# Attention with a capped MoE behind it: two units' sums from the exps, the last unit scaled early, products held back, late rows laid at once

## The chip, the cores and the metric

The kernel runs on one core of one Trainium2 chip. Its engines work side by side and wait for each other by semaphores: TensorE (PE in the profile; its weight loads are PEld), VectorE (DVE), ScalarE (ACT), GpSimd (POOL), and SyncE (SP), which issues most DMAs. The metric is the device time of one execution in microseconds, a median over runs.

## The reference

```python
def _attn_ref(q, k, v, cap):                       # 8 x 12 x 448 x 64
    scores = scale * np.matmul(q, k.transpose(0, 1, 3, 2))
    scores = cap * np.tanh(scores / cap)
    scores = scores - np.max(scores, axis=-1, keepdims=True)
    attn = np.exp(scores)
    attn = attn / (np.sum(attn, axis=-1, keepdims=True) + 1e-09)
    return np.matmul(attn, v)

def _moe_ref(x, w_gate, w1, w2, capacity):         # 3584 x 768, 8 experts, F 1024, capacity 80
    logits = x @ w_gate
    expert_idx = np.argmax(logits, axis=1)
    probs = softmax(logits)                        # written out there
    gate_w = probs[np.arange(N), expert_idx]
    out = np.zeros((N, D), dtype=np.float32)
    for e in range(E):
        tok_idx = np.where(expert_idx == e)[0]
        if len(tok_idx) > capacity:
            keep = np.argpartition(-gate_w[tok_idx], capacity)[:capacity]
            tok_idx = tok_idx[keep]
        h = np.maximum(x[tok_idx] @ w1[e], 0.0)
        out[tok_idx] = gate_w[tok_idx, None] * (h @ w2[e])
    return out
```

All 3584 tokens pass through attention and the gate. Of each expert only the tokens with the 80 highest gate weights pass through its two layers; all other rows of the output are zero.

## The kernel before

**Units.** Attention is cut into 24 units: a unit is four heads of one of the eight batches, three units a batch. For a unit TensorE computes the scores (`sc`, lines 1065 and 1073) in seven blocks of keys; ScalarE takes their tanh (line 1074) and exp (line 1078) into the tile `e`. One turn later TensorE multiplies `e` with V (`av`, line 1093, and the rests of the keys, line 1123) and with ones (`sp`, lines 1101 and 1121), which gives the softmax's row sums. To spare TensorE, GpSimd first adds the three full blocks of keys of each head pair (`esum`, tile `t`, lines 1084 and 1086), so that line 1101 multiplies one block instead of three. VectorE turns the sums into reciprocals (`sums`, tiles `st`, `rc`, `r`), scales `av` into `x` (`scaled`, line 1144) and transposes `x` into rows (`turned`, `xb`), which DMAs write to DRAM (`xs`).

**Order by hand.** The order of the work of one unit is the string `STEPS`: q scores, e exp, p GpSimd's sums, a the product with V, t the ones product over the blocks, r the rests, s reciprocals, n scaling, b a slot for the background. Behind the last unit `LAST` does the same, and there q is a step of the first expert's first layer (`begin`) and h makes a second copy of the ones (`again`: a matmul and a copy on ScalarE, `ones2`).

**Background.** After every third unit a gate runs: logits (`lgp`, line 1169), a transposition (`lt`, line 1183), the gate's small arithmetic on VectorE (`gate_math`, with a write of the gate weights `gd` at line 330), and the ranking of the batch's tokens. Ranking compares keys on VectorE (`gb`, line 414) and counts them with products of one column on TensorE (`pd`, line 420), whose result VectorE adds (`dfc`). These are steps in the lists `urgent`, `low` and `bg`, each with a cost in nanoseconds, a mark of what it does to a shared PSUM bank (`use`: 0 and 1 for TensorE's steps, -1 for the VectorE step that frees the bank) and a gap in slots. `background` hands them out in the slots; it keeps a model of TensorE's time (`clock[0]`) and VectorE's (`clock[1]`). In the last units such a step waits in the list while the model says that VectorE isn't there yet.

**Experts.** Six experts' rows are computed in the end. The rows of four are known from the first five batches: GpSimd gathers them by indirect DMAs (`xge`, line 708) and VectorE transposes them (`xt`, line 611). The last two experts wait for the last batch: `slots`, `compact` (`pcp` on TensorE, lines 681 and 684), `indices` (`ga`, `gi`, lines 689 and 692), the gathers `xgv` (three of 32 rows an expert, then the gate weights `gtv`), and `lay`, which transposes (line 1387), rounds on ScalarE (`xh`, line 1388) and subtracts (`xl`, line 1389). TensorE works through a list of 84 chunks (`hp` first layer, `yp` second layer, line 767); VectorE and ScalarE prepare two chunks ahead where weights are split into two parts (`whb` and `wha`, line 755; `wlb` and `wla`, line 757; `tlv`, line 806, is the same for the turned hidden rows). The `hp` tiles behind the first expert lie in the PSUM banks that `av` held.

The lines around the change, cut:

```python
STEPS = ("q0 e3 a00 b q1 q2 r0 b e0 p00 a10 a01 b q3 q4 r2 b e1 p01 t a11 b q5 r1 s q6 e2 p10 p11 a02 n0 a12 n1 b").split()
LAST = ("e3 a00 a10 q a01 a11 b r0 h q t b r2 a02 r1 s a12 q b q b q b q b").split()
```

Of the kernel before, what the change touches and what calls it, by code (L numbers as in the profile page):

```python
# [7 lines left out]
F32 = mybir.dt.float32  # L8
# [4 lines left out]
ALU = mybir.AluOpType  # L13
# [35 lines left out]
WMORE = 6  # L49
AHEAD = 2  # L50
WHOLE = (4, 3)
PLACE = (1900, 2300, 1900, 2400, 2000, 3500)
# [60 lines left out]
def attn_moe(ctx, tc, q2, k, v, cap, wg, w1, w2, capacity, ct, out):  # L113
# [875 lines left out]
    def vector(cost):  # L989

        clock[1] = max(clock) + cost
    st = {"laid": set(), "banks": ["misc"], "held": False}

# [24 lines left out]
    with ExitStack() as a2:  # L1018
# [77 lines left out]
        def total_of(u):  # L1096

            for i in range(2):
                for g in range(4):
                    w = slice(HQ * i, HQ * i + HQ)  # L1100
                    nc.tensor.matmul(st["sp", u][32 * g:32 * g + 32, w], ones[:, 0:32], st["es", u, g // 2][:, g % 2, w], start=False, stop=False)  # L1101

# [68 lines left out]
        def gate(b):  # L1171
# [14 lines left out]
            def math():  # L1186
                cs = slice(b * NC, (b + 1) * NC)
                lt = st["lt", b][:, :, :, 0:E]
                if b < OB:
                    st["math", b] = gate_math(sm, lt, b, kc[:, cs], oh[:, cs], b, us[:, cs], cms[:, cs])  # L1190
                else:
                    ws = slice(b * NC - OCOL, (b + 1) * NC - OCOL)
                    st["math", b] = gate_math(sm, lt, b, kc[:, cs], oh[:, cs], b, None, cmn[:, ws], ohv[:, ws], nc.sync if b < B - 2 else nc.scalar)
            def end(pd):
# [7 lines left out]
            def later():  # L1202
                st["math", b][2]()
                if b < OB:
                    steps = list(ranks(krow, gp, misc, b, acc, dfc, 0, 0, []))
                else:
                    steps = list(ranks(krow, gp, misc, b, acc2, dfc2, CAND, OCOL, [e * SL for e in range(E)]))
                if b == OB - 1:
                    kept = list(prune(krow, gp, misc))
                    n = next(i for i, x in enumerate(kept) if x[0] == 4000)  # L1210
                    steps = [*steps[0:2], kept[0], *steps[2:5], kept[1], *steps[5:8], kept[2], *steps[8:10], *kept[3:n], *steps[10:], *kept[n:]]
                bg.extend(apart(steps))
                now[2] = now[0]
                ready_at[2] = clock[1]
# [22 lines left out]
        def background(quota, took=2330, slack=1e9):  # L1237
# [6 lines left out]
            for q, last in ((urgent, 1), (low, 3), (bg, 2)):  # L1244
                while q and quota > 0:
                    cost, f, gap = q[0]
                    if gap == "ordered":
                        if not st.get("ordered"):
                            break
                        gap = 1  # L1250
                    n = getattr(f, "uses", None)
                    if n in (0, 1) and st["held"]:
                        break
                    if quota < 1e8:
                        if now[0] < now[last] + gap or (gap and n in (0, 1) and slack < 1e8 and clock[0] < ready_at[last]):
                            break
                        if max(clock) + cost > clock[0] + slack:
                            return
                    q.pop(0)
                    quota -= cost  # L1260
                    if n in (1, -1):
                        st["held"] = n == 1
                    vector(cost)
                    now[last] = now[0]
                    ready_at[last] = clock[1]
                    f()

        def laid(v):
# [22 lines left out]
        STEPS = ("q0 e3 a00 b q1 q2 r0 b e0 p00 a10 a01 b q3 q4 r2 b e1 p01 t a11 b q5 r1 s q6 e2 p10 p11 a02 n0 a12 n1 b").split()  # L1291
        LAST = ("e3 a00 a10 q a01 a11 b r0 h q t b r2 a02 r1 s a12 q b q b q b q b").split()
        TURNS = (1, 2, 3, 4, 5, 6, 0)
        RUNS = ((1, 3), (3, 5), (5, 7), (0, 1))
        for w in range(NU + 1):
# [15 lines left out]
            for i, x in enumerate(todo):  # L1311
# [9 lines left out]
                elif k_ == 'p':  # L1321
                    esum(w, *a_)
                elif k_ == 'a' and w:
# [7 lines left out]
                elif k_ == 'h':  # L1331
                    again()
                elif k_ == 'n' and 1 <= w < NU:
                    scaled(w - 1, a_[0])
                    if a_[0] == 1:
                        turned(w - 1, 0)
# [10 lines left out]
    st["banks"].append("sp")  # L1347
    for f in range(2):
        scaled(last_u, f)
    gate(B - 1)  # L1350
# [31 lines left out]
    def lay(v, i):  # L1382
        if i == 0:
            xv[v] = [fp.tile([128, KD, SL], d, name=f"x{k}{v}", tag=f"x{k}", bufs=n) for k, d, n in (("h", F32R, 2), ("l", F32R, 2), ("t", F32, 1))]
        xh, xl, xt = xv[v]
        w = slice(32 * i, 32 * i + 32)
        nc.vector.transpose(xt[:, :, w], fin["xg", v, i].rearrange("p (j c) -> p j c", c=32))
        nc.scalar.copy(xh[:, :, w], xt[:, :, w])
        nc.vector.tensor_tensor(xl[:, :, w], xt[:, :, w], xh[:, :, w].bitcast(F32), op=ALU.subtract)

    def chain():
# [3 lines left out]
        for v in range(NPRE, NV):  # L1395
            for i in range(3):
                bg.append((100, lambda v=v, i=i: fetch(v, i), 0))
            for i in range(3):
                bg.append((700, lambda v=v, i=i: lay(v, i), 3 * int(i == 0)))
        bg.append((800, lambda: fin.update(c=compare(fr, fin["tk"][:, 0:NPRE])), 0))  # L1400
# [101 lines left out]
```

## Time and profile before

| | us |
|---|---|
| median of 3 runs | 511.26 (510.77 to 513.09) |
| the profiled execution | 514.92 |
| its span, first to last instruction | 513.0 |
| TensorE busy | 478.0 (93%) |
| ScalarE busy | 364.2 (71%) |
| VectorE busy | 283.3 (55%) |
| GpSimd busy | 239.2 (47%) |
| mean granted TensorE clock | 0.981 |

The span is 1.9 us shorter than the execution. "Idle before" in brackets tells how long an engine stood before an instruction and what ended the wait; "issue" means that the profile shows nothing that ended it. A granted clock of 1.00 is 2.4 GHz, 0.5 is 1.2 GHz; a stretch that holds some of both shows a mean. Matmuls overlap, so the time that a group takes is the distance from its start to the next group's start. Fp32 matmuls leave two records each.

### The profile page before, as it was taken

To read this page: it belongs to the slowest core of one execution; us is meant where nothing else is said; L and a number is where in the kernel's file an instruction comes from. 1 tells how busy PE (TensorE), PEld (TensorE's weight loads), DVE (VectorE), ACT (ScalarE), POOL (GpSimd) and SP (SyncE) were. 2 spreads that over 40 slices of the span, in tenths; PEclk is the share of its full clock that TensorE was granted. 3 is DMA by queue.
4 is the path that set the end of the run, shared out by engine and by line. 5 is a ranking of instruction groups with operands and counts; after the bars stand their busy time and mean duration, and the time that the engine had idled before them with its cause. 6 is when DMAs were issued, how large, how long until landed. Compare 5 with 4: busy or idle time off the path is not lost.

```text
span 513.0 us, 18283 instructions
## 1 busy us (share of the span) xinstructions
PE 478.0 (93%) x7954; PEld 242.7 (47%) x7954; DVE 283.3 (55%) x753; ACT 364.2 (71%) x359; POOL 239.2 (47%) x164
## 2 busy tenths in 40 slices
PE   5799999999999999989999989999779999988992
PEld 1244444445444544444455435444334545545782
DVE  1033463365256556535878594587642747368881
ACT  4999899899889889968999978885011111256871
POOL 0666655646656656544665663587500014420000
PEclk9999999999999999989999999999989999998997
DMA  6966687685698668518456772945856889799820
GB/s 165 238 157 177 167 218 190 180 249 160 175 226 245 166 175 228 155 54 228 120 121 157 172 204 75 250 158 179 264 177 229 273 255 382 245 377 316 248 88 25
DMA packets 67608, 100.89 MB, mean 197 GB/s; under 512 B 12176, under 2 KB 49968, under 8 KB 67520
## 3 DMA queue, kind: packets, MB, share of 16 engines
q1 hardware_dynamic: 66016, 96.39, 64.8%
q0 software_dynamic: 1440, 3.25, 2.2%
q8 instruction: 64, 1.05, 0.9%
q14 instruction: 24, 0.20, 0.1%
q10 hardware_dynamic: 64, 0.00, 0.0%
HBM read 76.11 MB, written 23.80 MB: 195 GB/s over the span
## 4 chain that ended last, share of the span: by engine, by line
PE 79%; DVE 10%; DMA 4%; ACT 3%; issue 2%; SPq 1%; ACTq 0%; POOL 0%; POOLq 0%; DVEq 0%
PE sc L1073 22%; PE av L1093 19%; PE hp L767 10%; PE yp L767 7%; PE sp L1101 4%; PE av L1123 3%; PE lgp L1169 3%; PE sc L1065 3%; DMA w<-in_w_dram 2%; PE sp L1121 2%; PE pd L420 2%; ACT e L1074 2%; DVE x L1144 1%; DVE xb L1153 1%; DMA xge<-xs,gi 1%
## 5 line engine op out<-in xcount | busy, mean ns | idle before, releaser
L1074 ACT ACTIVATE e<-sc,scl 128x896 f32<-128x896 f32 x168 | 163.9, 1006 | 32.3 <-PE sc L1073 27.0
L1078 ACT ACTIVATE e<-e,capt 128x1792 f32<-128x1792 f32 x96 | 153.3, 1598 | 0.0
L1084 POOL TENSOR_TENSOR t<-e 128x896 f32<-128x896 f32 x48 | 101.1, 2107 | 99.8 <-ACT e L1078 98.7
L1073 PE MATMUL sc<-qt,kt 64*32 64x448 f32 x2304 | 134.7, 554 | 8.8 <-DMA qt<-in_q_dram 4.7
L1093 PE MATMUL av<-e,vr 128*32 128x224 f32 x2304 | 130.1, 359 | 2.4 <-DVE x L1144 2.4
L1086 POOL TENSOR_TENSOR t<-t,e 128x896 f32<-128x896 f32 x48 | 101.2, 2107 | 45.1 <-PE sc L1073 26.2
L1093 PEld LDWEIGHTS av<-e,vr 128*32 128x32 f32 x2304 | 67.8, 110 | 63.4 <-issue 20.1
L1131 DVE STREAM_TRANSPOSE st<-sp 128x448 f32<-128x448 f32 x24 | 15.5, 647 | 121.3 <-PE sp L1121 121.3
L1073 PEld LDWEIGHTS sc<-qt,kt 64*32 64x32 f32 x2304 | 32.8, 106 | 66.2 <-issue 42.4
L414 DVE TENSOR_SCALAR_CACHE_REDUCE gb<-krow,kc 112x896 bf16<-112x896 f32 (+16 forms) x59 | 52.6, 938 | 0.2 <-PE pd L420 0.2
L767 PE MATMUL hp<-w,xt 128*96 128x512 f32 x96 | 45.4, 618 | 2.7 <-issue 2.7
L824 POOL DMA_INDIRECT out_dram<-ysv,si x6 | 5.6, 938 | 83.4 <-ACT ysv L823 75.6
L1123 PE MATMUL av<-e,vr 64*32 64x224 f32 x384 | 41.2, 350 | 0.0
L1123 PE MATMUL av<-e,vx 64*32 64x224 f32 x384 | 40.9, 350 | 0.0
L767 PE MATMUL yp<-w,thv 128*96 128x384 f32 x96 | 32.3, 488 | 0.0
L1121 PE MATMUL sp<-e,ones 64*32 64x224 f32 x384 | 27.8, 350 | 2.8 <-ACT ones L1108 2.8
L1123 PEld LDWEIGHTS av<-e,vr 64*32 64x32 f32 x384 | 19.8, 107 | 21.9 <-issue 15.6
L1144 DVE TENSOR_TENSOR x<-av,r 128x448 f32<-128x448 f32 x48 | 27.7, 618 | 2.4
L1153 DVE STREAM_TRANSPOSE xb<-x 128x448 f32<-128x448 f32 x48 | 28.1, 624 | 0.8
L767 PEld LDWEIGHTS hp<-w,xt 128*96 128x96 f32 x96 | 15.2, 168 | 24.9 <-issue 24.9
L757 DVE TENSOR_TENSOR wlb<-w,whb 128x768 fp32r<-128x768 f32 x24 | 21.8, 952 | 4.8 <-ACT whb L755 4.4
L1101 PE MATMUL sp<-t,ones 128*32 128x224 f32 x384 | 23.5, 359 | 0.0
(263 smaller groups left out, 529.4 us busy)
## 6 DMA issues: line engine op xcount, KB each, us to landing
w<-in_w_dram SPq DMA_DIRECT2D x36, 512.0 KB
w<-in_w_dram SPq DMA_DIRECT2D x48, 384.0 KB
vr<-in_v_dram SPq DMA_DIRECT2D x24, 512.0 KB
out_dram<-zero SPq DMA_DIRECT2D x14, 768.0 KB
xs<-xb SPq DMA_DIRECT2D x32, 336.0 KB
kt<-in_k_dram SPq DMA_DIRECT2D x46, 224.0 KB
qt<-in_q_dram SPq DMA_DIRECT2D x46, 224.0 KB
vx<-in_v_dram SPq DMA_DIRECT2D x48, 32.0 KB
```

What stands on the lines that cost most here:

```text
L414: nc.vector.tensor_scalar(g, krow[:, x:y], kp, 0.0, op0=ALU.is_ge, op1=ALU.add, accum_out=a)
L767: nc.tensor.matmul(ps[nn][:, 0:m] if isinstance(ps, tuple) else ps[:, nn, 0:m], a[:, kk, :], bb[:, nn * m:(nn + 1) * m], start=(kk == 0 an ...
L1073: nc.tensor.matmul(ps[32 * m:32 * m + 32, h, :S], st["k", u][w, pr, y:y + 32], st["q", u][w, pr], start=True, stop=True)
L1074: nc.scalar.activation(st["e", u][:, 2 * x:2 * x + 2], ps[:, :, :S], AF.Tanh, scale=scl)
L1078: nc.scalar.activation(e, e, AF.Exp, scale=capt)
L1084: nc.gpsimd.tensor_tensor(t1, e[:, 0:2], e[:, 2:4], op=ALU.add)
L1086: nc.gpsimd.tensor_tensor(st["es", u, pr], st["es", u, pr], e[:, 4:6], op=ALU.add)
L1093: nc.tensor.matmul(st["av", u, i][32 * g:32 * g + 32, HQ * f:HQ * f + HQ], st["v", u][:, g // 2, g % 2, c, 32 * f:32 * f + 32], chunk_of(u ...
L1101: nc.tensor.matmul(st["sp", u][32 * g:32 * g + 32, w], ones[:, 0:32], st["es", u, g // 2][:, g % 2, w], start=False, stop=False)
L1121: nc.tensor.matmul(st["sp", u][32 * g:32 * g + 32, HQ * i:HQ * i + HQ], st["ones"][w, 0:32], e, start=(part == 0), stop=(part == 1))
L1123: nc.tensor.matmul(st["av", u, i][32 * g:32 * g + 32, HQ * f:HQ * f + HQ], last_of(u, pr, h, i)[w, 32 * f:32 * f + 32], e, start=False, st ...
L1153: nc.vector.transpose(st["xt", b][:, :, j, :], st["x", u][:, f].rearrange("p (a b) -> p a b", b=32))
```

## The change

1. Units 20 and 23 (`DIRECT`) have no sums by GpSimd. TensorE's ones product (`total_of`) takes the three blocks of exps itself, 24 matmuls instead of 8.
2. `LAST` scales the last unit (`n0 n1`) behind its last product with V, in the loop; before, it was done after the loop, behind what the lists had put on VectorE by then. The write of the gate weights of batch 6 goes from ScalarE's queue to SyncE's, and the small VectorE steps ahead of it move from the gate to behind the first count of that batch's ranking.
3. A TensorE step of the background on a shared bank (mark 0 or 1) now waits in its list, in every unit, until the model's TensorE time has reached the modelled end of the last VectorE step marked -1 and, where the step has a gap, the end of the list's last step. Before, this held for steps with a gap in the last units alone.
4. `lay` does an expert's three transposes and three roundings in one step and one subtraction over all 96 rows in a second one.

By 3 the counts' products of two batches stand further back on TensorE: those of the tenth unit's turn (`pd_6`) behind two more score blocks and rests, those of the sixteenth (`pd_14`) behind two products with V, two score blocks and rests. In the last units the logits and one transposition stand one slot later, and behind the last unit most products stand one chunk later, among them `pcp`.

```diff
@@ constants
+DIRECT = (20, 23)
@@ total_of
             for i in range(2):
-                for g in range(4):
-                    w = slice(HQ * i, HQ * i + HQ)
-                    nc.tensor.matmul(st["sp", u][32 * g:32 * g + 32, w], ones[:, 0:32], st["es", u, g // 2][:, g % 2, w], start=False, stop=False)
+                w = slice(HQ * i, HQ * i + HQ)
+                for c in range(NK if u in DIRECT else 1):
+                    for g in range(4):
+                        e = chunk_of(u, g // 2, c, g % 2)[:, w] if u in DIRECT else st["es", u, g // 2][:, g % 2, w]
+                        nc.tensor.matmul(st["sp", u][32 * g:32 * g + 32, w], ones[:, 0:32], e, start=False, stop=False)
@@ gate, math
-                    ... nc.sync if b < B - 2 else nc.scalar)
+                    ... nc.sync if b < B - 1 else nc.scalar)
@@ gate, later
-                st["math", b][2]()
+                if b != B - 2:
+                    st["math", b][2]()
...
-                bg.extend(apart(steps))
+                steps = apart(steps)
+                if b == B - 2:
+                    n = next(i for i, x in enumerate(steps) if i > 1 and getattr(x[1], "uses", None) == -1)
+                    steps.insert(n + 1, (1000, st["math", b][2], 0))
+                bg.extend(steps)
@@ background
-                        if now[0] < now[last] + gap or (gap and n in (0, 1) and slack < 1e8 and clock[0] < ready_at[last]):
+                        if now[0] < now[last] + gap or (n in (0, 1) and clock[0] < max(st["read"], ready_at[last] if gap else 0)):
                             break
...
                     f()
+                    if n == -1:
+                        st["read"] = clock[1]
@@ the loop over units
-        LAST = ("e3 a00 a10 q a01 a11 b r0 h q t b r2 a02 r1 s a12 q b q b q b q b").split()
+        LAST = ("e3 a00 a10 q a01 a11 b r0 h q t b r2 a02 r1 s a12 q n0 n1 b q b q b q b").split()
...
                 elif k_ == 'p':
-                    esum(w, *a_)
+                    if w not in DIRECT:
+                        esum(w, *a_)
...
-                elif k_ == 'n' and 1 <= w < NU:
+                elif k_ == 'n' and w:
                     scaled(w - 1, a_[0])
-                    if a_[0] == 1:
+                    if a_[0] == 1 and w < NU:
@@ after the loop
-    for f in range(2):
-        scaled(last_u, f)
@@ lay
-        w = slice(32 * i, 32 * i + 32)
-        nc.vector.transpose(xt[:, :, w], fin["xg", v, i].rearrange("p (j c) -> p j c", c=32))
-        nc.scalar.copy(xh[:, :, w], xt[:, :, w])
-        nc.vector.tensor_tensor(xl[:, :, w], xt[:, :, w], xh[:, :, w].bitcast(F32), op=ALU.subtract)
+        if i == 1:
+            nc.vector.tensor_tensor(xl, xt, xh.bitcast(F32), op=ALU.subtract)
+            return
+        for k3 in range(3):
+            w = slice(32 * k3, 32 * k3 + 32)
+            nc.vector.transpose(xt[:, :, w], fin["xg", v, k3].rearrange("p (j c) -> p j c", c=32))
+            nc.scalar.copy(xh[:, :, w], xt[:, :, w])
@@ chain
-            for i in range(3):
-                bg.append((700, lambda v=v, i=i: lay(v, i), 3 * int(i == 0)))
+            bg.append((1500, lambda v=v: lay(v, 0), 3))
+            bg.append((700, lambda v=v: lay(v, 1), 1))
```

How the built order of the engines changes is shown at three places; line numbers are those of each kernel, so after the change they are up to 14 higher. First ScalarE behind the last unit's exps, before the change: `tau` belongs to the gate of batch 6, `gd` is the write of its weights, `ones` the second copy of the ones.

```order
L1078 ACTIVATE e_5413<-e_5413,capt 128x1792
L1078 ACTIVATE e_5413<-e_5413,capt 128x896
L304 ACTIVATE tau_5643<-d_5642 112x32
L330 DMA gd<-grow 4x32 x3
L330 DMA gd<-grow 4x16
L1108 COPY ones_5739<-ones_5737 128x32
L396 COPY krow<-psk_5802 112x448
```

And after the change:

```order
L1079 ACTIVATE e_5423<-e_5423,capt 128x1792
L1079 ACTIVATE e_5423<-e_5423,capt 128x896
L305 ACTIVATE tau_5647<-d_5646 112x32
L1111 COPY ones_5732<-ones_5730 128x32
L397 COPY krow<-psk_5816 112x448
```

The write of the gate's weights no longer stands ahead of the copy of the ones.

Second VectorE in the same place, before: `gb` are compares for the counts, `xt_3` the transposes of the fourth early expert's rows, `x` the scaling of the last unit, `dfc` the addition of the first counts.

```order
L407 SCALAR_TENSOR_TENSOR gl_3_5816,acc_95<-psk_5802,kc,ctt 112x112
L414 TENSOR_SCALAR gb_0_5820,acc_95<-krow,kc 112x880
L414 TENSOR_SCALAR gb_1_5822,acc_95<-krow,kc 112x896
L414 TENSOR_SCALAR gb_1_5822,acc_95<-krow,kc 112x96
L611 STREAM_TRANSPOSE xt_3_115<-xge_0_5795 128x6x32
L611 STREAM_TRANSPOSE xt_3_115<-xge_1_5797 128x6x32
L611 STREAM_TRANSPOSE xt_3_115<-xge_2_5799 128x6x32
L1144 TENSOR_TENSOR x_5852<-av_0_5673,r_5780 128x2x224
L1144 TENSOR_TENSOR x_5852<-av_1_5682,r_5780 128x2x224
L428 TENSOR_TENSOR dfc_96<-dfc_96,pd_0_5830 112x9
```

And after:

```order
L1147 TENSOR_TENSOR x_5801<-av_1_5686,r_5789 128x2x224
L612 STREAM_TRANSPOSE xt_2_114<-xge_0_5637 128x6x32
L612 STREAM_TRANSPOSE xt_2_114<-xge_1_5639 128x6x32
L612 STREAM_TRANSPOSE xt_2_114<-xge_2_5641 128x6x32
L408 SCALAR_TENSOR_TENSOR gl_0_5824,acc_95<-psk_5816,kc,ctt 112x112
L408 SCALAR_TENSOR_TENSOR gl_1_5826,acc_95<-psk_5816,kc,ctt 112x112
L408 SCALAR_TENSOR_TENSOR gl_2_5828,acc_95<-psk_5816,kc,ctt 112x112
L408 SCALAR_TENSOR_TENSOR gl_3_5830,acc_95<-psk_5816,kc,ctt 112x112
L612 STREAM_TRANSPOSE xt_3_115<-xge_0_5807 128x6x32
L612 STREAM_TRANSPOSE xt_3_115<-xge_1_5809 128x6x32
L612 STREAM_TRANSPOSE xt_3_115<-xge_2_5811 128x6x32
L415 TENSOR_SCALAR gb_0_5837,acc_95<-krow,kc 112x880
```

The scaling went ahead of both early experts' transposes, and the fourth expert's transposes went ahead of the compares. On TensorE the logits and the first counts now stand behind the second expert's first chunk.

Third VectorE at the late rows, before: `rh` is an operand of `pcp`, `ga` to `sg` the lists of rows, `tlv` a part of the turned hidden rows of the fourth expert.

```order
L671 TENSOR_TENSOR rh<-oh_90,bo 112x12x24
L689 TENSOR_SCALAR ga<-pcp 32x18
L692 TENSOR_SCALAR gi<-ga 32x18 x4
L699 TENSOR_SCALAR sz<-sa 96x6
L700 TENSOR_SCALAR sa<-sa 96x6
L701 TENSOR_TENSOR si<-sa,sz 96x6
L702 TENSOR_SCALAR sg<-sa 96x6
L806 TENSOR_TENSOR tlv_6508<-htv_6506,thv_6507 128x768
L1387 STREAM_TRANSPOSE xt_6551<-xgv_0_6519 128x6x32
L1389 TENSOR_TENSOR xl_6550<-xt_6551,xh_6549 128x6x32
```

And after:

```order
L672 TENSOR_TENSOR rh<-oh_90,bo 112x12x24
L807 TENSOR_TENSOR tlv_6510<-htv_6508,thv_6509 128x768
L690 TENSOR_SCALAR ga<-pcp 32x18
L693 TENSOR_SCALAR gi<-ga 32x18 x4
L700 TENSOR_SCALAR sz<-sa 96x6
L701 TENSOR_SCALAR sa<-sa 96x6
L702 TENSOR_TENSOR si<-sa,sz 96x6
L703 TENSOR_SCALAR sg<-sa 96x6
L1400 STREAM_TRANSPOSE xt_6575<-xgv_0_6543 128x6x32
L1400 STREAM_TRANSPOSE xt_6575<-xgv_1_6545 128x6x32
L1400 STREAM_TRANSPOSE xt_6575<-xgv_2_6547 128x6x32
L758 TENSOR_TENSOR wlb_0_6586<-w_6_6355,whb_0_6584 128x768
```

`tlv` went ahead of the lists, and the three transposes stand together ahead of the first `wlb`.

## Rows read from the trace of the kernel before

**Rows 1.** Stretch; busy us of PE, PEld, DVE, ACT, POOL (x instructions); clock; DMA share; GB/s.

```profile
20.00:300.00 280.00, 276.81 (x5968) 134.91 (x5968) 150.47 (x426) 255.77 (x235) 166.63 (x80) 0.99 0.68 181
```

**Rows 2.** TensorE's waits, whole run: us in all, times, longest.

```profile
PE sp L1121 <- ACT ones L1108: 2.8, 1, 2.8
...
PE pd L420 <- DVE gb L414: 2.6, 3, 1.1
...
PE lgp L1169 <- DVE tab L572: 0.4, 1, 0.4
```

**Rows 3.** Granted clock (PEclk) in four stretches, same view as rows 1.

```profile
220.00:225.00 5.00, 4.45 (x64) 2.16 (x72) 0.66 (x3) 0.74 (x1) 2.08 (x1) 0.66 0.09 21
...
305.00:310.00 5.00, 4.73 (x68) 1.59 (x72) 4.93 (x8) 1.79 (x3) 2.82 (x2) 0.66 1.04 269
...
362.00:367.00 5.00, 2.17 (x42) 0.85 (x35) 1.96 (x10) 0.18 (x1) 2.02 (x3) 1.00 0.55 153
...
377.00:382.00 5.00, 4.92 (x8) 1.83 (x9) 2.99 (x9) 0.00 (x0) 0.00 (x0) 0.66 0.12 28
```

**Rows 4.** Timeline of VectorE, unit 20: start, us, line, operation, tiles, sizes.

```profile
296.22 2.02 DVE L506 TENSOR_TENSOR r<-r,os 112x20 f32<-112x20 f32 x1
...
299.80 2.90 DVE L551 TENSOR_TENSOR prlh<-r,ctt 112x768 bf16<-112x768 f32 x1
...
306.88 2.31 DVE L551 TENSOR_TENSOR prlh<-r,ctt 112x768 bf16<-112x768 f32 x2
```

**Rows 5.** Timeline of GpSimd, the same stretch.

```profile
299.78 2.10 POOL L1086 TENSOR_TENSOR t<-t,e 128x896 f32<-128x896 f32 x1 [1.57 <-PE sc L1073]
```

**Rows 6.** Timeline of TensorE, units 20 and 21; in brackets idle time before.

```profile
305.27 1.30 PE L1093 MATMUL av<-e,vr 128*32 128x224 f32 x16 [1.94 <-DVE x L1144]
...
313.53 0.96 PE L1101 MATMUL sp<-t,ones 128*32 128x224 f32 x16
...
314.31 0.94 PE L1093 MATMUL av<-e,vr 128*32 128x224 f32 x16
```

**Rows 7.** Timeline of all engines behind the last unit.

```profile
359.46 1.33 PE L1101 MATMUL sp<-t,ones 128*32 128x224 f32 x16
...
366.49 1.96 PE L767 MATMUL hp<-w,xt 128*96 128x512 f32 x4
...
370.46 1.12 DVE L414 TENSOR_SCALAR_CACHE_REDUCE gb<-krow,kc 112x880 bf16<-112x880 f32 x1
...
373.82 0.57 PE L420 MATMUL pd<-ones_b,gb 112*128 112x1 bf16 x17
...
375.55 0.38 DVE L611 STREAM_TRANSPOSE xt<-xge 128x192 f32<-128x192 f32 x1 [0.89 <-DMA xge<-xs,gi]
...
375.86 1.12 DVE L1144 TENSOR_TENSOR x<-av,r 128x448 f32<-128x448 f32 x2
...
377.07 5.34 PE L767 MATMUL hp<-w,xt 128*96 128x512 f32 x8 [2.68 <-issue]
...
383.01 1.70 PE L1169 MATMUL lgp<-x,wgt 128*32 128x448 f32 x12
```

**Rows 8.** Timeline of VectorE, ScalarE and TensorE, late rows; last the gathers' landing.

```profile
438.98 0.17 DVE L689 TENSOR_SCALAR ga<-pcp 32x18 f32<-32x18 f32 x1 [3.57 <-PE pcp L684]
...
444.99 0.96 DVE L806 TENSOR_TENSOR tlv<-htv,thv 128x768 fp32r<-128x768 f32 x1 [2.05 <-ACT thv L805]
...
448.07 0.37 DVE L1387 STREAM_TRANSPOSE xt<-xgv 128x192 f32<-128x192 f32 x1
...
448.73 1.56 ACT L755 CAST whb<-w 128x768 fp32r<-128x768 f32 x2
...
451.35 0.81 PE L767 MATMUL yp<-whb,thv 128*96 128x384 f32 x2
...
464.98 0.96 DVE L757 TENSOR_TENSOR wlb<-w,whb 128x768 fp32r<-128x768 f32 x1
...
DMA to landing us min/median/max: 3.7/5.2/6.7
```

More of the change, by code (lines that the diff above doesn't have):

```diff
@@ L991, in vector @@
         clock[1] = max(clock) + cost
-    st = {"laid": set(), "banks": ["misc"], "held": False}
+    st = {"laid": set(), "banks": ["misc"], "held": False, "read": 0}
     def use(n, f):
@@ L1192, in math @@
                     ws = slice(b * NC - OCOL, (b + 1) * NC - OCOL)
-                    st["math", b] = gate_math(sm, lt, b, kc[:, cs], oh[:, cs], b, None, cmn[:, ws], ohv[:, ws], nc.sync if b < B - 2 else nc.scalar)
+                    st["math", b] = gate_math(sm, lt, b, kc[:, cs], oh[:, cs], b, None, cmn[:, ws], ohv[:, ws], nc.sync if b < B - 1 else nc.scalar)
             def end(pd):
```

## The prediction

> **What bounds the kernel now.** I read the busy time by stretch first. From 20 to 300 us TensorE is busy 276.8 of 280 us and ScalarE 255.8 [rows 1]: TensorE bounds these units, and ScalarE is close behind. So only two things can shorten the run: a wait of TensorE itself, or less work on it.
>
> The view of waits comes next. Beside its start, TensorE waits 2.6 us in three places for the rank compares before the counts' products (`pd`), 2.8 us for one small copy on ScalarE (`ones2`), and twice 0.4 us for a bank [rows 2] (one of the two is shown). The timeline adds 1.94 us at 305.27 for a scaled sum (`x`) [rows 6] and 2.68 us at 377.07 [rows 7]. The page names no releaser for that last one; the tile `hp` of the second expert lies in the banks of `av`, and the row that ends just before it is the scaling `x<-av` that empties them, in line behind transposes waiting for gathered rows.
>
> Third, the clock. Behind the waits that end at 220.8, 305.3 and 377.1 the granted clock is 0.66 over 5 us, so 1.7 us at full speed are lost each time at the lower of its two levels (1.2 instead of 2.4 GHz). A window with 2.8 us of waiting at 362 to 367 kept 1.00 [rows 3]. So a wait of 1.5 us or more can cost 1.7 us on top, but need not.
>
> **The change part by part.** The sum is made against the profiled execution, 514.92 us, of which 513.0 are span. It is 3.7 us above the median of the runs, 511.26, and I subtract the same sum from the median.
>
> (a) Counts' products. A product now stays back until the modelled end of the compares that it reads. In the built order the two that waited (1.08 us, and 0.74 twice) stand behind four to five more microseconds of matmuls, so the 2.6 us of [rows 2] go, and with them the half-speed stretch at 220 [rows 3]. What comes next on DVE there has slack. −2.6 − 1.7 = **−4.3 us**. If ScalarE took over the wait this would be 0, if the clock fell anyway −2.6.
>
> (b) Sums of unit 20. TensorE adds three chunks instead of one: 16 records take 0.78 us from 313.53 to 314.31 [rows 6], 48 take 2.34, so +1.56. Nothing hides it. Against it, four adds of 2.1 us leave POOL. DVE's small step at 296.22 lasts 2.02 us where its like take 0.2, and the next long one 2.90 us where two of the same form take 2.31 together [rows 4]; both end as POOL's adds end (299.78 + 2.10) [rows 5]. Without the adds DVE is at least 3.6 us earlier (1.8 + 1.75), and `x` is there before TensorE asks at 303.3. The wait of 1.94 and the half-speed stretch at 305 go: −1.9 − 1.7 + 1.6 = **−2.0 us**. Its ends: +1.6 if the wait has another cause, −2.1 if the matmuls overlap a little more. The bank waits (lgp, and the transposes after it) stand one slot later: −0.8 us.
>
> (c) The last unit. Take TensorE from the sums at 359.46 to the first matmul of the second expert at 377.07, 17.6 us [rows 7]. Now: sums 2.34; what lies between them and 366.49, 7.03 less the 2.83 of waiting [rows 2] and the old sums' 1.33, so 2.9, since ScalarE's copy no longer stands behind the gate's DMAs; four chunks of the first expert and a transposition, 366.49 to 373.82, 7.3. That is 12.5, so the second expert starts 5.1 us earlier, at 372.0; `x`, 1.1 us of scaling [rows 7], follows the unit's reciprocals at once, some 5 us ahead of that, and no longer holds it.
>
> But a wait comes in its place. DVE now does the last early transposes before the compares, where before they followed. These wait for a gather that can start only when the transposes just before them free its buffers, 367.3, about as before, so they end at 375.2 (375.93 before) [rows 7]. The compares for `pd` then take 2.4 us (two like the 1.12 of [rows 7] and a short one) and end at 377.6. TensorE, with its first chunk (1.7, a quarter of the 7.3 less a transposition) and the logits (1.7) [rows 7] done, stands at 375.4. The products' 0.57 stood ahead before and stand here now, so the second chunk starts at 377.7 instead of 376.0: −5.1 + 0.6 + 1.7 = −2.8 us. The half-speed stretch at 377 goes or comes back behind this wait: −4.5 or −2.8, and I take **−3.6 us**, since waits of 1.5 and 2.8 us have gone either way [rows 3].
>
> (d) The late rows. The list of the last two experts is now one slot later on TensorE, and DVE stands to do `tlv` before `ga`, where it did `ga` first. `ga` moves from 438.98 to 445.95, when `tlv` (444.99 + 0.96) ends [rows 8]: 7.0 us. The gathers follow it at once, so the third row block's transposition, at 448.07 before, comes at 455.0 if the landing takes as long. The cast `whb` behind it starts 0.66 later and lasts 0.8 [rows 8], so the first split chunk is there at 456.5, and TensorE asks for it at 451.35: a new wait of 5.1 us. DVE bounds what follows. Before, from that cast's end (449.5) to the last `wlb` (464.98 + 0.96) 16.4 us went by. Now its work is eight `wlb` at 0.87 (7.0), two subtractions over all columns at 0.7 (1.4), three transposes (0.9), 1.2 until the casts behind them have let `whb` through, and 2.5 of small compares: 13.0. So laying in one go saves 3.4 us, and its end is at 469.5 instead of 465.9: **+3.6 us**. Landings here take 3.7 to 6.7 us [rows 8], which gives +2.0 to +5.0; the half-speed stretch that follows at 466 stays, and a second one is +1.7.
>
> The Trainium skill has a price for such a gather: DMA: Bandwidth & Descriptors, section Anatomy of one DMA, gives 2.0 us and a size term, for 98 KB an estimate of 2.2 us in all. The trace's shortest landing is 3.7 [rows 8], so here the measurement decides; by the page (d) would be 3.0 less than by the median landing of 5.2, so +0.6, and the time 501.2 us.
>
> (e) The gate's small DMAs move from ScalarE's queue to SP's, between two weight loads. The loads behind them wait for the gate's last step; no wait of TensorE in the view is for a weight load, so it costs nothing until that lead is gone. The write of the last rows moves back by one load: nothing either. POOL's and ScalarE's freed time is off the path.
>
> Sum: −4.3 − 2.0 − 0.8 − 3.6 + 3.6 = −7.1. The profiled execution would take 507.8, the median **504.2 us**.
>
> **The rivals.**
> A, short landing. The late gathers land in 3.7 us, because TensorE's new wait lets the weight stream run dry: (d) is +2.0, and with it the clock stays up in (c), another −0.9: 501.7 us. For it: landing was 3.7 for the first of them. Against: 5 to 7 for the later ones.
> B, clock unchanged. The lower level comes back somewhere for each removed wait, because the new waits in (c) and (d) take their place: +1.7 twice and +0.9, so 508.5 us. For it: (d)'s wait is longer than any before. Against: between 20 and 350 us no new wait stands.
> C, ScalarE takes the waits. Between 20 and 345 us ScalarE becomes the bound as soon as TensorE no longer waits, so (a), the 3.6 us won in (b) and the 0.8 give nothing: −7.1 + 8.7 = +1.6, so 512.9 us, slower than before. It decides where ScalarE has less idle time in those units than TensorE's wait that goes; over 280 us it has 24.2, some 1.2 a unit [rows 1], and around 305 and 220 it was itself waiting for TensorE. So little speaks for it.
> D, the change doesn't do what it says. DVE's long steps at 296 to 302 are not POOL's doing, and unit 20 only pays: (b) is +1.6 for −2.0: 507.8 us. The ends of both steps at the ends of POOL's adds speak against it.
>
> **How the numbers follow.** The forecast, 502 to 507 us around 504.2, has 0.58; A 0.12, B 0.17, C 0.06, D 0.07. The range 500.5 to 509.0 holds the forecast, A, B and D, and leaves out C and the longest landings with a second slow stretch. What a measurement tells from no change is about 0.5%, 2.6 us: faster means under 508.7, which holds the forecast, A, D and half of B, 0.85; B's other half and part of C lie within, 0.11; slower has 0.04.
>
> **What would show it.** In the profile after: no wait of TensorE for `gb` between 120 and 225 us, and clock 1.00 at 220 and 305; POOL without adds in units 20 and 23, DVE's steps there at a tenth of their length; the totals at 2.3 us a unit; `ones2` copied within a microsecond of its matmul; TensorE waiting 1 to 2 us for `gb` behind the logits; and a wait of 4 to 6 us for `whb` at the first split chunk. If that last wait is missing, (d) is wrong and the time is near 501; if TensorE waits for ScalarE's `e` in units that had no such wait, C is right.

## The result, and the profile after

The changed kernel takes 505.79 us (median of 4 runs, 505.71 to 507.43), the kernel before beside it 511.74 us (510.77 to 513.09): a ratio of 0.989 (95% interval 0.9858 to 0.9921), by which it is 5.6 us less. Two further sets gave 0.9908 (0.9873 to 0.9942) and 0.9915 (0.9887 to 0.9944), 4.4 to 4.8 us less. Runs over 1.5% above the fastest of the same kernel count as slow and are left out of all ratios: three of the kernel before in the first set (516.3 to 517.0 us) and one of u_math_sc (793.8 us, at a mean clock of 0.56). The forecast was 504.2 us, 7.1 less. Its direction, places and order of size held; the run gained somewhat less than forecast, the two profiled executions more: 514.92 and 505.72 us, 9.2 less.

TensorE's starts in the two traces place the 9.5 us by which its last matmul ends earlier (503.55 and 494.05 us):

| TensorE reaches | before | after | change there | forecast |
|---|---|---|---|---|
| first product with V | 18.22 | 18.61 | +0.4 | 0 |
| turn 15, behind the two places of (a) | 234.08 | 229.78 | −4.7 | −4.3 |
| turn 21, behind unit 20 and its sums (b) | 320.79 | 314.38 | −2.1 | −2.0 |
| turn 23 (bank waits) | 351.58 | 343.99 | −1.2 | −0.8 |
| asks for the first `whb` (c) | 451.35 | 439.14 | −4.6 | −3.6 |
| end (d) | 503.55 | 494.05 | +2.7 | +3.6 |

The stretches of the trace after that answer to [rows 1] and [rows 3] (same columns), and the stretch in which the clock falls now:

```profile
20.00:300.00 280.00, 279.42 (x6072) 136.22 (x6064) 153.39 (x435) 260.33 (x239) 164.60 (x78) 1.00 0.69 183
220.00:225.00 5.00, 5.00 (x149) 3.17 (x141) 0.38 (x2) 4.08 (x4) 3.42 (x2) 1.00 0.01 3
305.00:310.00 5.00, 5.00 (x116) 3.29 (x108) 0.00 (x0) 3.23 (x3) 3.44 (x2) 1.00 0.18 65
443.00:448.00 5.00, 2.96 (x9) 2.61 (x10) 3.36 (x5) 4.07 (x6) 3.53 (x4) 0.52 0.70 221
```

Between 20 and 300 us TensorE's idle time went from 3.2 to 0.6 us; the clock stays at 2.4 GHz until the late rows. TensorE's waits after, which answer to [rows 2] (us in all, times, longest):

```profile
PE yp L768 <- ACT whb L756: 5.9, 1, 5.9
...
PE yp L768 <- DVE wlb L758: 1.9, 2, 1.6
PE pd L421 <- DVE gb L415: 1.1, 2, 0.7
PE lt L1186 <- ACT krow L584: 0.8, 1, 0.8
PE av L1094 <- DVE x L1147: 0.4, 1, 0.4
```

The wait for the ones is gone; the 1.1 us for `gb` are not the old ones, but the new pair behind the logits. In unit 20 VectorE's two steps that lasted 2.02 and 2.90 us [rows 4] now take a tenth and a third of that. The first of the two scalings `x` at 297.80 ends at 298.42, half a microsecond before TensorE's product with V at 298.97, which waits for nothing. The totals are three times as long as in [rows 6]:

```profile
291.92 0.18 DVE L507 TENSOR_TENSOR r<-r,os 112x20 f32<-112x20 f32 x1
...
293.64 0.95 DVE L552 TENSOR_TENSOR prlh<-r,ctt 112x768 bf16<-112x768 f32 x1
...
297.80 1.16 DVE L1147 TENSOR_TENSOR x<-av,r 128x448 f32<-128x448 f32 x2
```

```profile
298.97 0.96 PE L1094 MATMUL av<-e,vr 128*32 128x224 f32 x16
...
305.60 2.48 PE L1104 MATMUL sp<-e,ones 128*32 128x224 f32 x48
307.89 0.94 PE L1094 MATMUL av<-e,vr 128*32 128x224 f32 x16
```

Behind the last unit (against [rows 7]) the ones are copied at once, `x` follows its reciprocals, the second expert's first chunk runs without a wait as the last four of the twelve records at 360.99, and the compares come behind the fourth expert's transposes:

```profile
350.16 0.19 ACT L1111 COPY ones<-ones 128x32 f32<-128x32 f32 x1 [1.39 <-PE ones L1109]
...
351.82 2.48 PE L1104 MATMUL sp<-e,ones 128*32 128x224 f32 x48
...
358.28 1.16 DVE L1147 TENSOR_TENSOR x<-av,r 128x448 f32<-128x448 f32 x2
...
360.99 5.32 PE L768 MATMUL hp<-w,xt 128*96 128x512 f32 x12
...
366.24 1.70 PE L1172 MATMUL lgp<-x,wgt 128*32 128x448 f32 x12
366.85 0.38 DVE L612 STREAM_TRANSPOSE xt<-xge 128x192 f32<-128x192 f32 x1 [1.21 <-DMA xge<-xs,gi]
367.15 1.09 DVE L415 TENSOR_SCALAR_CACHE_REDUCE gb<-krow,kc 112x880 bf16<-112x880 f32 x1
...
368.30 0.35 PE L421 MATMUL pd<-ones_b,gb 112*128 112x1 bf16 x8 [0.36 <-DVE gb L415]
```

At the late rows (against [rows 8]) `ga` stands behind `tlv`, the third transposition ends at 443.87, the cast follows, and TensorE waits 5.90 us (forecast 5.1):

```profile
432.32 0.96 DVE L807 TENSOR_TENSOR tlv<-htv,thv 128x768 fp32r<-128x768 f32 x1 [7.87 <-ACT thv L806]
433.19 0.15 DVE L690 TENSOR_SCALAR ga<-pcp 32x18 f32<-32x18 f32 x1
...
443.49 0.38 DVE L1400 STREAM_TRANSPOSE xt<-xgv 128x192 f32<-128x192 f32 x1 [1.42 <-DMA xgv<-xs,gi]
...
444.16 1.56 ACT L756 CAST whb<-w 128x768 fp32r<-128x768 f32 x2
...
445.04 0.95 PE L768 MATMUL yp<-whb,thv 128*96 128x384 f32 x2 [5.90 <-ACT whb L756]
...
458.04 0.42 PE L768 MATMUL yp<-wlb,thv 128*96 128x384 f32 x1 [1.62 <-DVE wlb L758]
```

### The profile page after: what moved, and what is told of

Same layout as the page of the kernel before. It is cut to its first block, busy times and chain, and to the rows that moved or that the text cites. A ratio compares the mean times of both kernels' runs of the same rounds, so it can differ in the third digit from the quotient of the medians.

```text
span 503.4 us, 18394 instructions
## 1 busy us (share of the span) xinstructions
PE 475.0 (94%) x8018; PEld 244.2 (49%) x8018; DVE 273.4 (54%) x749; ACT 363.6 (72%) x359; POOL 223.0 (44%) x156
## 4 chain that ended last, share of the span: by engine, by line
PE 88%; DMA 4%; ACT 3%; DVE 2%; issue 1%; SPq 0%; POOL 0%; POOLq 0%; ACTq 0%; DVEq 0%
PE sc L1074 24%; PE av L1094 23%; PE hp L768 9%; PE yp L768 8%; PE sp L1104 5%; PE av L1126 4%; PE sc L1066 3%; PE lgp L1172 2%; PE pd L421 2%; PE sp L1124 2%; DMA xgv<-xs,gi 2%; ACT e L1075 2%; ACT e L1079 1%; PE yp5a L768 1%; DMA xge<-xs,gi 1%; PE yp5b L768 1%
## 5 line engine op out<-in xcount | busy, mean ns | idle before, releaser
L1085 POOL TENSOR_TENSOR t<-e 128x896 f32<-128x896 f32 x44 | 92.8, 2110 | 106.8 <-ACT e L1079 105.8
L1087 POOL TENSOR_TENSOR t<-t,e 128x896 f32<-128x896 f32 x44 | 92.8, 2108 | 39.2 <-PE sc L1074 19.1
L768 PE MATMUL hp<-w,xt 128*96 128x512 f32 x96 | 43.9, 597 | 0.0
L1066 PE MATMUL sc<-qt,kt 64*32 64x224 f32 x768 | 23.1, 349 | 0.0
```

What stands on the lines that cost most here:

```text
L768: nc.tensor.matmul(ps[nn][:, 0:m] if isinstance(ps, tuple) else ps[:, nn, 0:m], a[:, kk, :], bb[:, nn * m:(nn + 1) * m], start=(kk == 0 an ...
L1066: nc.tensor.matmul(ps[32 * m:32 * m + 32, h, HQ * pr:HQ * pr + HQ], st["k", u][w, pr, y:y + 32], st["q", u][w, pr, HQ * i:HQ * i + HQ], st ...
L1085: nc.gpsimd.tensor_tensor(t1, e[:, 0:2], e[:, 2:4], op=ALU.add)
L1087: nc.gpsimd.tensor_tensor(st["es", u, pr], st["es", u, pr], e[:, 4:6], op=ALU.add)
```

## The experiments

The runs come in three sets: c_before to u_late, c_after to e_flag, and the rest. The changed kernel was not run in the first set, so the runs there are set against it by their ratios to the kernel before. In the second and third set the kernel before is 6 us longer than in the first, and the changed kernel 8 to 10 us longer than in its first measurement. The eight traces of these sets, all of variants of the changed kernel, show a part of it: from the transposition `lt` near 324 us (the one that waits for `krow`) to the matmul for the ones TensorE takes 32.3 to 34.5 us, in the six other traces 25.4 to 26.1. Waits without a releaser make up 0.9 to 3.0 us of that stretch; where the rest goes stays open. So each run is compared within its set where that can be done.

| run | median us | before, same set | ratio (95%) |
|---|---|---|---|
| c_before | 514.04 | 513.84 | 1.000 (0.997 to 1.003) |
| u_products | 510.85 | 513.84 | 0.9956 (0.9930 to 0.9981) |
| u_math | 503.81 | 513.84 | 0.9827 (0.9787 to 0.9867) |
| u_late | 506.66 | 513.84 | 0.9881 (0.9841 to 0.9921) |
| c_after | 513.85 | 519.90 | 0.9908 (0.9873 to 0.9942) |
| u_sums | 513.05 | 519.90 | 0.9896 (0.9860 to 0.9932) |
| u_scale | 519.93 | 519.90 | 1.0018 (0.9991 to 1.0045) |
| e_flag | 508.77 | 519.90 | 0.9813 (0.9779 to 0.9846) |
| c_after2 | 515.75 | 520.42 | 0.9915 (0.9887 to 0.9944) |
| best_0 | 509.13 | 520.42 | 0.9784 (0.9751 to 0.9817) |
| best_20 | 508.55 | 520.42 | 0.9779 (0.9749 to 0.9810) |
| u_math_sc | 510.40 | 520.42 | 0.9805 (0.9763 to 0.9846) |

**c_before and c_after: the kernels unchanged.**

> The kernel before, unchanged, to see how its runs differ. Theory: its profiled execution of 514.92 us lies 3.7 us above the median because TensorE's lower clock level was granted for one or two stretches of 3.4 us more than in the usual run (1.7 us lost by each); runs near 511 us then show a mean clock of 0.985 to 0.988, runs above 513 us 0.981 to 0.983, and a trace of a run near 511 us lacks one or two of the four half-speed stretches at 220, 306, 377 and 466 us. Rival: the stretches are the same in all runs (mean clock 0.981 in each) and the waits differ.

> The changed kernel, unchanged, beside the others of this set. Theory: its time spreads less than the kernel before's (which ran from 508.3 to 516 us), since it has fewer waits behind which the clock can fall: 505.7 to 508 us, median 506. Rival: the spread comes from elsewhere and stays 6 us or more.

Half of the first theory fell. In that set the kernel before ran from 508.3 to 515.6 us, but in c_before the mean clock doesn't sort its runs: 510.98 us came with 0.981, 515.08 with 0.983. Its new trace ends 4.2 us earlier than the old one. At 219 us it has the same waits for `gb` (0.74 us twice) and no slow clock behind them (compare 0.66 in [rows 3]); later it lost the half-speed stretch at 377 and got a longer one at 363:

```profile
220.00:225.00 5.00, 4.41 (x100) 2.32 (x104) 0.70 (x3) 2.17 (x3) 2.10 (x1) 1.00 0.16 47
...
363.00:369.00 6.00, 5.56 (x36) 2.01 (x37) 2.56 (x8) 0.18 (x1) 1.75 (x2) 0.50 0.76 254
```

So whether the clock falls behind a given wait differs from run to run, and some waits differ too (at 375 us 0.5 us where [rows 7] have 2.7). The changed kernel spreads less than the kernel before each time, but with fewer runs or as few: 505.7 to 507.4, 512.8 to 514.2 and 514.2 to 516.2 us (n = 4, 6, 6), against 510.8 to 513.1, 515.8 to 521.5 and 516.9 to 523.2 (n = 4, 17, 11). So the smaller spread is likely and not shown. The size of c_after's forecast was missed by 8 us, in a set in which the kernel before is 6 us longer too.

**u_products: the old rule for the counts' products.**

```
-  if now[0] < now[last] + gap or (n in (0, 1) and clock[0] < max(st["read"], ready_at[last] if gap else 0)):
+  if now[0] < now[last] + gap or (gap and n in (0, 1) and slack < 1e8 and clock[0] < ready_at[last]):
```

> The changed kernel with the old rule for the counts' products. Theory: the waits for gb near 130 and 219 us come back (1.1 and 0.7 + 0.7 us, with one half-speed stretch), the new wait of 1.1 us at 368 us goes since the compares stand ahead of the fourth expert's transposes again: 505.8 + 2.6 + 1.7 - 1.1 = 509.0 us, 507.3 without the half-speed stretch. Rival: the products were never the limit there and ScalarE takes the waits over: 505.8 us, within 0.7.

The three waits for `gb` are back and the new pair near 368 us is gone, as expected; those for the banks (0.36 and 0.42) are back too. Its trace ends at 499.0 us, 5.0 behind the changed kernel's. In the ratio the rule is worth 0.4 to 0.7 points, 2 to 3.5 us: about the wait, with little of the clock. Its interval lies above that of the changed kernel's first measurement and overlaps the two others. This trace too shows 1.00 at the waits at 219 us. ScalarE takes nothing over. The view of waits and the stretch in u_products:

```profile
PE pd L421 <- DVE gb L415: 2.6, 3, 1.1
...
219.00:224.00 5.00, 3.52 (x78) 2.12 (x86) 2.19 (x5) 2.28 (x2) 3.40 (x2) 1.00 0.40 114
```

**u_sums: units 20 and 23 from GpSimd.** `DIRECT = ()`.

> The changed kernel with the sums of units 20 and 23 made by GpSimd again. Theory: 24 matmuls less in each unit (-1.56 us twice), the wait of 1.9 us for x near 299 us comes back, with or without a half-speed stretch (1.7 us): -3.1 + 1.9 = 1.2 us less than the changed kernel, or 0.5 more with the stretch: 504.8 to 506.5 us. Rival: VectorE's long steps in unit 20 were not GpSimd's doing, no wait comes back, and 3.1 us are saved: 502.7 us.

The cause was right and the bargain poor. VectorE's long steps return, the first ends with GpSimd's add (294.73 and 294.69), the second 0.8 us, nearly its own length, behind the next add's end (299.19 and 298.37); the prediction had let it end with the add. TensorE waits again:

```profile
292.71 2.02 DVE L507 TENSOR_TENSOR r<-r,os 112x20 f32<-112x20 f32 x1
...
296.29 2.90 DVE L552 TENSOR_TENSOR prlh<-r,ctt 112x768 bf16<-112x768 f32 x1
```

```profile
292.59 2.10 POOL L1085 TENSOR_TENSOR t<-e 128x896 f32<-128x896 f32 x1 [1.04 <-ACT e L1079]
296.27 2.10 POOL L1087 TENSOR_TENSOR t<-t,e 128x896 f32<-128x896 f32 x1 [1.58 <-PE sc L1074]
```

```profile
301.76 1.35 PE L1094 MATMUL av<-e,vr 128*32 128x224 f32 x16 [1.94 <-DVE x L1147]
```

Behind this wait the clock is at its lower level here; behind the same wait in best_0 it is not (first u_sums, then best_0):

```profile
302.00:305.50 3.50, 3.50 (x48) 1.16 (x48) 3.46 (x5) 0.61 (x1) 2.31 (x2) 0.53 1.09 265
...
299.00:304.00 5.00, 3.45 (x76) 1.61 (x80) 4.83 (x8) 3.19 (x4) 4.12 (x2) 1.00 1.05 244
```

The Trainium skill (SBUF — State Buffer, Who interferes with whom) says that a VectorE instruction with two SBUF inputs contends with a GpSimd instruction that reads SBUF, and that such contention is an exclusive lock. The traces agree: 0.18 us for `r<-r,os` without the adds, 2.02 beside one, and it ends with the add. This kernel's median is 0.8 us below c_after's, but the intervals overlap, so no gain of the direct sums is shown and no loss either: two units' extra matmuls cost some 3 us and buy a wait of 1.9 and, where the clock falls, 1.7.

**u_scale: the last unit scaled behind the compares.** `n0 n1` out of `LAST`, the two calls of `scaled` after the loop.

> The changed kernel with the last unit scaled after the loop again, behind the compares. Theory: the second expert's first chunk, asked for near 364.5 us, waits for x, which ends some 1.2 us behind the compares at 369.5: a wait of 6.1 us, less the 1.1 us of waiting for gb that go: 5.0 us more than the changed kernel, 511 us, 1.7 more if the clock falls. Rival: the banks of av were not what the second expert waited for (the profile of before named no releaser), and it is 506 us as with the scaling ahead.

6.1 us more than c_after (1.0018 against 0.9908): the gain of the whole change is gone. `x` ends at 378.53 and the second expert's first chunk follows 0.1 us later, at half speed (3.55 us for four records that take 1.94 elsewhere):

```profile
377.38 1.15 DVE L1147 TENSOR_TENSOR x<-av,r 128x448 f32<-128x448 f32 x2
378.63 3.55 PE L768 MATMUL hp<-w,xt 128*96 128x512 f32 x4 [4.92 <-issue]
```

**u_late: laying in three parts.**

```
-  bg.append((1500, lambda v=v: lay(v, 0), 3))
-  bg.append((700, lambda v=v: lay(v, 1), 1))
+  for i in range(3):
+      bg.append((700, lambda v=v, i=i: lay(v, i), 3 * int(i == 0)))
...
```

The body of `lay` is that of the kernel before.

> The changed kernel with the late rows laid in three parts again, as before (nine steps for an expert instead of seven, each part's subtraction by itself). Theory of the prediction: VectorE's work from the first whb to the last wlb is 16.4 us instead of 13.0, so 3.4 us more: 509.2 us, and the wait for the first whb stays near 5.9 us. Rival: the parts are done while later gathers land, and nearly nothing is lost: 506.5 us or less.

The rival held. By the ratio (0.9881) nothing is lost, and the trace ends 0.8 us behind the changed kernel's. For the second expert's rows VectorE needs three times 1.2 us instead of 1.65 in all, 1.9 us more. But an expert's list is a step longer, and that pushes the flag's small compares (`fn` to `fl_i`) behind the last `wlb`, where they cost little:

```profile
456.64 0.96 DVE L758 TENSOR_TENSOR wlb<-w,whb 128x768 fp32r<-128x768 f32 x1
457.52 0.15 DVE L848 TENSOR_TENSOR fn<-nesk,nesn 1x8 f32<-1x8 f32 x1
```

In the changed kernel they stand ahead of it, 1.7 us from 455.33 on, and TensorE's wait of 1.62 us at 458.04 follows. From the first `whb` to the last `wlb` it is 13.0 us in both. Laying at once saved on VectorE what the compares then took in its place. So the 3.4 us between the 16.4 of the kernel before and 13.0 are not laying's alone: u_late, with the old laying, is rid of them too, of 1.7 us by the flag's compares and of 1.7 by VectorE's wait for the third `whb`, 0.42 us where it was 2.14 (first the kernel before, then u_late). What laying at once is worth with the compares in one place wasn't tried.

```profile
453.55 0.96 DVE L757 TENSOR_TENSOR wlb<-w,whb 128x768 fp32r<-128x768 f32 x1 [2.14 <-ACT whb L755]
...
446.86 1.83 DVE L758 TENSOR_TENSOR wlb<-w,whb 128x768 fp32r<-128x768 f32 x2 [0.42 <-ACT whb L756]
```

**u_math and u_math_sc: the gate's last small steps back in the gate; in the second the weights written from ScalarE's queue as well.**

```
-  if b != B - 2:
-      st["math", b][2]()
+  st["math", b][2]()
...
-  steps.insert(n + 1, (1000, st["math", b][2], 0))
```

> The changed kernel with the gate's last small steps for batch 6 back in the gate (its weights still written from SyncE's queue). Theory: the extra step in the list is what put the lists of the late rows one slot later and behind tlv; with ga ahead of tlv the gathers start some 5 us earlier, TensorE's wait of 5.9 us for whb shrinks to under 1.5 us, and VectorE's 13.0 us from the first whb to the last wlb bound what follows: some 4 us less than the changed kernel, 501.8 us (500 to 503.5). Rival: the wait is the gathers' landing beside the weight stream, which only moves: 504.5 us or more.

> The changed kernel with the gate's last small steps back in the gate and the gate's weights written from ScalarE's queue again, so the copy of the ones stands behind four DMAs. Theory: TensorE waits 2.8 us for the ones again; the wait behind it for gb (2.6 us where only the small steps are back) goes, since TensorE comes later and gb does not: 0.2 us more than with the small steps back alone, whose trace ends at 491.2 us, and no wait for gb at 367 us. Rival: both waits stand, 2.8 us more.

u_math settles where the late lists' place comes from. The rule for the products doesn't set it: with the old rule (u_products) `ga` still stands behind `tlv`. The step inserted for the gate does. It belongs to part 2 of the change; the section on the change names part 3 for the later place of `pcp`, and that is wrong: behind `pcp` TensorE still has a chunk of the first layer to do in the kernel before and in u_math, and none in the changed kernel and in u_products. Without that step `ga` runs at 428.55 instead of 433.19, the first `whb` is there when asked for, and the wait that remains is a shorter one three chunks on:

```profile
440.93 0.81 PE L768 MATMUL yp<-whb,thv 128*96 128x384 f32 x2
...
447.53 0.59 PE L768 MATMUL yp<-whb,thv 128*96 128x384 f32 x2 [2.80 <-ACT whb L756]
```

By the ratios it is 0.6 to 0.9 points faster than the changed kernel, 3 to 4.5 us, as expected, though its interval overlaps the first of the changed kernel's three and its wait for `gb` at 367 us grew to 2.6 us.

In u_math_sc no wait for the ones came back, against the expectation. ScalarE issues the four DMAs at 357.76 and copies the ones at 359.58, but TensorE needs them only behind the totals, which end at 365.21:

```profile
357.76 1.77 ACTq L331 DMA_DIRECT2D gd<-grow  x4
...
359.58 0.19 ACT L1111 COPY ones<-ones 128x32 f32<-128x32 f32 x1 [4.98 <-PE ones L1109]
...
362.32 2.89 PE L1104 MATMUL sp<-e,ones 128*32 128x224 f32 x48
```

Before, the DMAs went out at 362.98, since the gate's arithmetic ran later: one of its steps lasted 2.06 us and ended as GpSimd's add for unit 23 ended (359.84 and 359.79).

```profile
357.78 2.06 DVE L296 SCALAR_TENSOR_TENSOR cand<-d,ctt 112x32 f32<-112x32 f32 x1
...
357.71 2.08 POOL L1086 TENSOR_TENSOR t<-t,e 128x896 f32<-128x896 f32 x1
```

The queue alone was not what held the copy. GpSimd's adds alone weren't either: u_sums has them back, with the write on SyncE's queue, and its trace shows no wait for the ones. How the gain divides among the earlier arithmetic, the missing adds and the longer totals wasn't tried apart.

**e_flag, best_0, best_20, c_after2: a faster version.** The lists one slot earlier, the flag's compares eight slots later; then units 20 and 23, or 23 alone, back to GpSimd.

```
-  bg.append((1500, listed, 2))
+  bg.append((1500, listed, 1))
...
-  bg.append((1500, lambda: flag(fr, fin["c"]), 0))
+  bg.append((1500, lambda: flag(fr, fin["c"]), 8))
```

> The changed kernel with the lists of the late rows one slot earlier (gap 1 instead of 2, so ga stands ahead of tlv) and the last eight small compares of the flag eight slots later. Theory: the wait of 5.9 us for the first whb shrinks to under 1.5 us, and the two waits of 0.4 and 1.6 us for wlb at 455 to 458 us go; VectorE's 11.5 us from the first whb to the last wlb still bound that stretch, so about 5 us less than the changed kernel: 500.5 us (499 to 502). Rival: the flag's small steps are no part of it and the gain is that of the earlier lists alone, 2 to 3 us: 503.5 us.

> The changed kernel once more, as the base that the other runs of this set are compared with: 505.7 to 508 us if the set is as the first, 513 to 514 if as the second; its share of the kernel before 0.989 to 0.991.

> The earlier lists and the later flag (e_flag), with all units' sums from GpSimd. Theory: against e_flag 3.1 us of matmuls go and the wait of 1.9 us for x in unit 20 comes back: 1.2 us less than e_flag, or 0.5 more where the clock falls behind that wait; so 6.3 us less than the changed kernel, or 4.6. Rival: with unit 23's sums from GpSimd the last totals wait for GpSimd, and it is 2 us or more slower than best_20.

> The earlier lists and the later flag (e_flag), with unit 20's sums from TensorE and unit 23's from GpSimd again. Theory: only unit 20 had a wait to pay for the extra matmuls, unit 23's 1.56 us bought nothing: 1.6 us less than e_flag, so 6.7 us less than the changed kernel. Rival: unit 23's totals come to wait for GpSimd's adds, and nothing is gained over e_flag (5.1 us less than the changed kernel).

e_flag is 5.1 us faster than c_after, as expected; its waits for `whb` are 2.5 us in two places instead of 5.6 in one, and those for `wlb` are gone. What the later flag adds to the earlier lists was not tried apart: u_math, with the lists early and the flag where it was, has a ratio inside e_flag's interval. best_20 is 7.2 us faster than c_after2, best_0 6.6. Between these two no difference is shown, and e_flag's 5.1 in another set lies near them, so unit 23's extra matmuls probably bought nothing and unit 20's hardly pay. best_20 is 2.2% faster than the kernel before (1.9 to 2.5) and beats the changed kernel by 1.4%; its largest wait behind the start is

```profile
PE yp L768 <- ACT whb L756: 2.1, 1, 2.1
```

## Why the prediction was right, point by point

- (a) held in place and size in the trace (−4.7 for −4.3). u_products shows the wait as the lasting part, 2 to 3.5 us; the 1.7 us of clock were in one of three traces with these waits.
- (b) held: VectorE's stall is GpSimd's, which u_sums shows in both directions, so rival D falls. The price of 1.56 us a unit was nearly exact: 48 records take 2.29 us from 305.60 to 307.89, 1.5 more than 16. Only the first of VectorE's two long steps ended with an add, not both. The clock part was there in three of four traces with that wait: the kernel before twice, u_sums, but not best_0. That the bargain as a whole pays is not shown (u_sums against c_after, best_0 against best_20).
- (c) held: the second expert started some 5 us earlier, as worked out, and the new wait for `gb` is 1.1 us for 1.7. The clock stayed up behind it, so −4.6, the better of the two ends. u_scale shows the scaling as the heart of it. The reason given for the ones is incomplete: ScalarE's queue alone brings no wait back (u_math_sc).
- (d) held for the wait and not for what follows. TensorE waits 5.9 us for 5.1, as the order of `tlv` and `ga` sets it. VectorE's 13.0 us from the first `whb` (444.96) to the last `wlb` (457.99) are the forecast's number, but not by its reason: it let laying in one go save 3.4 us of the 16.4, and u_late, which lays in three parts, takes 13.0 as well. Up to the matmul behind that `wlb` (465.99 before, 458.04 after) the late rows cost 4.3 us; 1.5 came back behind it, where the half-speed stretch that the forecast kept at 466 is missing. The lower clock level now stands behind the new wait (443 to 448). The slot was named rightly as the cause of the order, the part of the change that sets it wrongly (u_math).
- (e) held: no wait of TensorE for a weight load.
- Rival C falls: ScalarE is busy 260.3 us of 280 and no unit waits for `e` beyond the start. Rival A's short landing was there for single gathers (2.7 us), but the median was 5.0, and none landed in the estimated 2.2. Rival B falls in the trace: the clock came down behind one of the new waits, that of (d), and not behind that of (c).
- That the number came so near is luck in part. The sum was made for the profiled execution and was too small there: 507.8 forecast, 505.72 measured. Taken off the median it was too large: 504.2 forecast, 505.79 measured. The changed kernel's profile lies at its median, the kernel before's 3.7 us above, and the sum took the half-speed stretches of that one execution in full, 1.7 + 1.7 + 0.9. Counted by the share of traces in which they stand, one in three for (a) and three in four for (b), the sum would be −5.5, an estimate from few traces. That the clock accounts for the 1.6 us is not shown: in c_before the mean clock does not sort the runs.

## What to carry to other kernels

Count a wait that goes at its own length, and the clock's part behind it by how often several traces show it; one profile is one draw. In a planner of slots, a step put into a list moves everything behind it: look first for who stands ahead of the instruction that the next long chain hangs on. Here the lists one slot earlier and the flag's compares eight later were worth 5 us together. Work taken off a helper engine is paid on the engine that bounds, so do it at most in the unit whose wait it removes; here even there the gain is not clear of the noise.

## What the runs showed of the hardware that was not expected

Behind the same two waits of 0.74 us near 220 us the granted clock fell in one trace (0.66 over 5 us) and stayed at 2.4 GHz in two; behind the wait of 1.94 us in unit 20 it fell in three of four. Behind the wait of 5.5 to 6.1 us at the late rows it was at the lower level, 0.50 over 3 us, in all seven traces that have it. And TensorE can be held by something that the profile doesn't name: in every trace of the second and third set the stretch from near 324 us to the matmul for the ones took 32.3 to 34.5 us, with waits of up to 0.85 us each that have no releaser, where the six other traces took 25.4 to 26.1 and show no such wait there.
